# A decode kernel of two attention and two GLU layers: batches in two groups with K and V resident, K turned by VectorE

## The chip, the cores and the metric

The kernel runs on one core of a Trainium2 chip. All times are device microseconds (us) of one execution. A run more than 1.5% above the fastest of its kernel is called slow and is left out of the ratios. Medians are quoted over all runs, slow ones included, so where the two differ the ratio is to be trusted. "Granted clock" is the share of full speed at which TensorE's array clock runs, as the profile records it.

The profile names the engines PE (TensorE matmuls), PEld (TensorE weight loads), DVE (VectorE), ACT (ScalarE), POOL (GpSimd) and SPq (the queue of the sync engine, which issues all DMA here).

## The reference

Four tokens (batch 4, one position each, width 512) pass four layers: attention, GLU, attention, GLU. Both attentions use the same K and V caches and the same weights, and so do both GLUs.

```python
def attention(x):                       # x: [4, 1, 512]
    q = x @ wq                          # 32 heads of 128; 8 K/V heads, each shared by 4 query heads
    k, v = the last W = 2048 positions of k_cache, v_cache      # [4, 8, 2048, 128] each
    p = softmax(q k^T * 128 ** -0.5)
    return (p v) @ wo                   # [4096, 512]
def glu(x):
    return (sigmoid(x @ w_gate) * (x @ w_up)) @ w_down          # 512 -> 1792 -> 512
x = x + attention(layernorm(x)); x = x + glu(layernorm(x))
x = x + attention(layernorm(x)); x = x + glu(layernorm(x))
```

A (head, batch) pair has 512 KiB (0.52 MB) of K and as much of V; there are 32 pairs. K and V together are 33.6 MB. The kernel keeps an arena in on-chip memory of 49 slots of 512 KiB each, 25.7 MB, so K and V do not fit in it all at once. The second attention needs the result of the first for the same batch, but not for other batches: this is what the change uses.

## The kernel before

Every step is recorded as an operation with an engine, an assumed duration and the tiles that it reads and writes. A list scheduler then fixes the order on each engine, and semaphore waits are derived. Loads are issued in a fixed order; each takes the next free slot.

```python
# (cut) order of the layers
q_proj(0, ...)
for h in range(HKV):                    # first attention, all four batches of a head together
    if h + 1 < HKV: k_transpose(h + 1)
    scores_softmax(0, [h], QB, OB)
    pv_wo(0, h, keep)                   # V is dropped, K stays in its slots
glu(1)
q_proj(2, units2)
for hs in units2:                       # second attention: K is resident, V is loaded again
    scores_softmax(2, hs, 4, 5)
    ...
glu(3)
```

K is turned by TensorE transposes into PSUM, evacuated by VectorE and ScalarE in turn. In the scores, four neighbouring matmuls write to four column groups of the array (PSUM partitions 0, 32, 64, 96):

```python
for i, h in enumerate(heads):
    for b in range(NB):                 # b picks the column group
        pe.matmul(ps[32 * b:32 * b + rows, c, :], qt[:, q0:q0 + rows], K[h, b][:, c * 512:(c + 1) * 512], ...)
```

In the GLU, gate and up go to two PSUM banks, and each weight tile is one operation of 14 matmuls with four moving columns:

```python
for c in range(NC):
    for nm, bank in (("g", GB), ("u", UB)):
        P.op("tensor", ..., r=slot_tok(s) + [("xn",)], w=[("psg", bank)], banks=(bank,))
```

## Time and profile before

| | |
|---|---|
| time | 210.2 us (median of 3 runs; 208.6 to 211.6) |
| span of the profiled run | 207.9 us |
| read from HBM | 73.9 MB |
| PE / DVE / ACT busy | 69% / 35% / 32% |
| middle: end of attention 1 to first scores of attention 2 | 118.5 to 142.7 us, 24 us |
| end: end of attention 2 to the end of the span | 195.3 to 207.9 us, 12.6 us |

The first lines are the row of granted clock, the row of mean DMA busy share (both in tenths) and the GB/s moved, in 40 equal slices of 5.2 us, from the page of the kernel before:

```profile
PEclk9955588596699676969975555555555555555555
DMA  5999999999999999999997799999999999999300
GB/s 204 348 414 412 411 391 408 398 405 404 392 408 390 407 394 405 402 395 411 391 363 261 240 359 300 419 409 407 408 409 408 411 404 407 406 405 368 121 3 1
...
HBM read 73.93 MB, written 0.00 MB: 356 GB/s over the span
```

Outside three places (the start, the middle GLU in slices 21 to 25, the last four slices) DMA moves 390 to 419 GB/s. The kernel before is paced by its loads.

Some of the costliest groups of the same page (line, engine, operation, output and input tiles, shapes, count, then busy us and mean ns of one, then the idle time before them):

```profile
L526 PE MATMUL ps<-ident_b,arena 128*128 128x128 bf16 x512 | 48.5, 260 | 12.3 <-ACT arena L537 5.0
L537 ACT COPY arena<-ps 128x1024 bf16<-128x1024 bf16 x32 | 32.4, 1011 | 45.8 <-PE ps L526 45.8
...
L607 DVE TENSOR_REDUCE nmax<-ps 128x1 f32<-128x2048 f32 x12 | 27.5, 2290 | 11.8 <-PE ps L598 11.8
...
L598 PE MATMUL ps<-arena,qpad 128*8 128x512 bf16 x128 | 15.5, 617 | 0.8 <-DVE qpad L577 0.8
...
L598 PE MATMUL ps<-arena,qflat 128*4 128x512 bf16 x128 | 13.8, 481 | 0.5 <-DVE qflat L565 0.5
```

The transposes of K (L526) are the largest group. The 256 score matmuls (L598) are busy for 29.3 us together although one takes 481 or 617 ns: several run at once.

Two lines of the timeline: the middle GLU's gate and up, and the first score block of attention 2. A line gives start and duration in us, then instructions of one kind merged and their count, and in brackets the idle time of the engine before them and what ended it ("issue": nothing that the profile shows).

```profile
121.25 3.13 PE L710 MATMUL ps<-xn,arena 128*128 128x4 bf16 x112 [1.43 <-DVE xn L505]
...
142.68 3.59 PE L598 MATMUL ps<-arena,qpad 128*8 128x512 bf16 x32 [0.81 <-DVE qpad L577]
```

### The profile page before, as it was taken

To read this page: it belongs to the slowest core of one execution; us is meant where nothing else is said; L and a number is where in the kernel's file an instruction comes from. 1 tells how busy PE (TensorE), PEld (TensorE's weight loads), DVE (VectorE), ACT (ScalarE), POOL (GpSimd) and SP (SyncE) were. 2 spreads that over 40 slices of the span, in tenths; PEclk is the share of its full clock that TensorE was granted. 3 is DMA by queue.
4 is the path that set the end of the run, shared out by engine and by line. 5 is a ranking of instruction groups with operands and counts; after the bars stand their busy time and mean duration, and the time that the engine had idled before them with its cause. 6 is when DMAs were issued, how large, how long until landed. Compare 5 with 4: busy or idle time off the path is not lost.

```text
span 207.9 us, 6311 instructions
## 1 busy us (share of the span) xinstructions
PE 143.3 (69%) x2872; PEld 110.4 (53%) x2872; DVE 71.7 (35%) x155; ACT 67.1 (32%) x103; POOL 1.4 (1%) x9
## 2 busy tenths in 40 slices
PE   1684885969969499797756662547296972967564
PEld 1683554858657477675625662443054740546563
DVE  4410262363363534637435220201414204142221
ACT  2430146283584372938354010000314103131000
POOL 2000000000000000000000000000000000000000
PEclk9955588596699676969975555555555555555555
DMA  5999999999999999999997799999999999999300
GB/s 204 348 414 412 411 391 408 398 405 404 392 408 390 407 394 405 402 395 411 391 363 261 240 359 300 419 409 407 408 409 408 411 404 407 406 405 368 121 3 1
DMA packets 26409, 74.33 MB, mean 358 GB/s; under 512 B 2312, under 2 KB 10000, under 8 KB 26384
## 3 DMA queue, kind: packets, MB, share of 16 engines
q1 hardware_dynamic: 26384, 73.94, 92.6%
q8 instruction: 22, 0.36, 0.7%
q14 instruction: 3, 0.02, 0.0%
HBM read 73.93 MB, written 0.00 MB: 356 GB/s over the span
## 4 chain that ended last, share of the span: by engine, by line
PE 36%; SPq 24%; DMA 16%; DVE 12%; ACT 7%; issue 4%; ACTq 0%; DVEq 0%
SPq L367 24%; PE ps L598 10%; PE ps L659 9%; DVE nmax L607 8%; DMA arena<-in_A_k_cache_dram 8%; PE ps L526 7%; DMA arena<-in_A_wq_dram 5%; ACT prow L611 5%; DMA arena<-in_B_w_down_dram 4%; PE ps L684 2%; PE ps L619 2%; PE ps L710 2%; PE ps L639 2%; PE ps L740 1%; ACT arena L537 1%
## 5 line engine op out<-in xcount | busy, mean ns | idle before, releaser
L526 PE MATMUL ps<-ident_b,arena 128*128 128x128 bf16 x512 | 48.5, 260 | 12.3 <-ACT arena L537 5.0
L526 PEld LDWEIGHTS ps<-ident_b,arena 128*128 128x128 bf16 x512 | 39.4, 119 | 22.3 <-issue 10.5
L537 ACT COPY arena<-ps 128x1024 bf16<-128x1024 bf16 x32 | 32.4, 1011 | 45.8 <-PE ps L526 45.8
L611 ACT ACTIVATE prow<-ps,nmax 128x1024 bf16<-128x1024 f32 x24 | 26.6, 1113 | 46.7 <-DVE nmax L607 46.6
L659 PE MATMUL ps<-ebuf,arena 128*128 128x4 bf16 x1024 | 29.5, 166 | 7.4 <-DVE xT L691 5.2
L659 PEld LDWEIGHTS ps<-ebuf,arena 128*128 128x128 bf16 x1024 | 28.6, 102 | 11.1 <-issue 11.0
L607 DVE TENSOR_REDUCE nmax<-ps 128x1 f32<-128x2048 f32 x12 | 27.5, 2290 | 11.8 <-PE ps L598 11.8
L533 DVE COPY arena<-ps 128x1024 bf16<-128x1024 bf16 x32 | 22.1, 689 | 26.8 <-PE ps L526 26.8
L619 PE MATMUL ps<-sel_b,prow 128*128 128x16 bf16 (+1 forms) x192 | 8.9, 178 | 15.2 <-ACT prow L611 15.0
L619 PEld LDWEIGHTS ps<-sel_b,prow 128*128 128x128 bf16 x192 | 7.0, 101 | 21.9 <-ACT prow L611 17.9
L553 PE MATMUL ps<-xn,arena 128*128 128x4 bf16 x256 | 9.3, 167 | 10.4 <-DMA arena<-in_A_wq_dram 8.4
L598 PE MATMUL ps<-arena,qpad 128*8 128x512 bf16 x128 | 15.5, 617 | 0.8 <-DVE qpad L577 0.8
L553 PEld LDWEIGHTS ps<-xn,arena 128*128 128x128 bf16 x256 | 8.3, 105 | 11.6 <-DMA arena<-in_A_wq_dram 9.5
L598 PE MATMUL ps<-arena,qflat 128*4 128x512 bf16 x128 | 13.8, 481 | 0.5 <-DVE qflat L565 0.5
L671 DVE TENSOR_TENSOR onb<-ps,rinv 128x16 bf16<-128x16 f32 x16 | 3.1, 194 | 30.1 <-PE ps L659 30.1
L684 PEld LDWEIGHTS ps<-onb,arena 128*128 128x128 bf16 x256 | 8.4, 104 | 5.6 <-DVE onb L671 4.1
L684 PE MATMUL ps<-onb,arena 128*128 128x4 bf16 x256 | 9.3, 167 | 1.7 <-DVE onb L671 1.7
L499 ACT ACTIVATE lnv<-lnv 128x4 f32<-128x4 f32 x4 | 0.8, 205 | 27.3 <-DVE lnv L496 27.3
L710 PE MATMUL ps<-xn,arena 128*128 128x4 bf16 x224 | 6.3, 166 | 2.8 <-DVE xn L505 2.8
L740 PE MATMUL ps<-hT,arena 128*128 128x4 bf16 x112 | 4.1, 166 | 5.9 <-DMA arena<-in_B_w_down_dram 2.9
L710 PEld LDWEIGHTS ps<-xn,arena 128*128 128x128 bf16 x224 | 6.1, 104 | 3.0 <-issue 3.0
L629 ACT CAST ebuf<-ps 128x256 bf16<-128x256 f32 (+1 forms) x12 | 5.4, 449 | 6.9 <-PE ps L619 6.9
(45 smaller groups left out, 55.8 us busy)
## 6 DMA issues: line engine op xcount, KB each, us to landing
arena<-in_A_v_cache_dram SPq DMA_DIRECT2D x64, 512.0 KB, 12.3
arena<-in_A_k_cache_dram SPq DMA_DIRECT2D x32, 512.0 KB, 12.7
arena<-in_A_wq_dram SPq DMA_DIRECT2D x16, 512.0 KB, 10.8
arena<-in_A_wo_dram SPq DMA_DIRECT2D x8, 512.0 KB, 15.0
arena<-in_B_w_gate_dram SPq DMA_DIRECT2D x8, 448.0 KB, 12.4
arena<-in_B_w_up_dram SPq DMA_DIRECT2D x8, 448.0 KB, 9.4
arena<-in_B_w_down_dram SPq DMA_DIRECT2D x6, 512.0 KB, 9.6
arena<-in_B_w_down_dram SPq DMA_DIRECT2D x2, 256.0 KB, 7.5
```

The lines of the kernel that those rows point to most:

```text
L367: o = P.op("sync", name, 0.0, lambda e, dst=dst, src=src: e.dma_start(dst, src), r=r, w=w, dma_bytes=nbytes, dma_rate=tm[rate])
L526: last = pe.transpose(bankb(bank)[:, j * 128:(j + 1) * 128], half[:, j * 128:(j + 1) * 128], ident_b[:, :])
L533: lambda v, half=half, bank=bank: v.tensor_copy(half, bankb(bank)[:, 0:TB * 128]),
L537: lambda a, half=half, bank=bank: a.copy(half, bankb(bank)[:, 0:TB * 128]),
L553: last = pe.matmul(ps[:, QB, q * NB:(q + 1) * NB], src[:, k * 128:(k + 1) * 128], xn[:, c * NB:(c + 1) * NB], start=(st and k == 0), stop= ...
L598: last = pe.matmul(ps[32 * b:32 * b + rows, c, :], qt[:, q0:q0 + rows], slot_ap(s)[:, c * CH:(c + 1) * CH], start=(i == 0), stop=(i == ni ...
L607: lambda v: v.tensor_reduce(nm, ps[:, 0:NCH, :].rearrange("p c n -> p (c n)"), AXX, ALU.max, negate=True),
L611: lambda a, t=t: a.activation(prow[:, t * 1024:(t + 1) * 1024], ps[:, 2 * t:2 * t + 2, :].rearrange("p c n -> p (c n)"), ACTF.Exp, bias=nm ...
L619: last = pe.matmul(ps[:, ptb, j * n:(j + 1) * n], prow[:, j * 128:(j + 1) * 128], sel_b[:, 0:n], start=True, stop=True)
L659: last = pe.matmul(ps[:, OB, b * REP:(b + 1) * REP], src[:, j * 128:(j + 1) * 128], ebuf[:, c0:c0 + REP], start=(j == 0), stop=(j == NJ - 1))
L684: last = pe.matmul(ps[:, OB, 64 + c * NB: 64 + (c + 1) * NB], slot_ap(s)[:, r_ * D + c * 128:r_ * D + (c + 1) * 128], ov[:, r_ * NB:(r_ + ...
L710: last = pe.matmul(ps[:, bank, fc * NB:(fc + 1) * NB], src[:, fc * 128:(fc + 1) * 128], xn[:, c * NB:(c + 1) * NB], start=(c == 0 and fc = ...
```

## The change

The intent is to read V once. Batches are split into two groups, [0, 1] and [2, 3]. A group's K and V (16 pairs, 32 slots) stay resident through attention 1, GLU, and attention 2. The order becomes: attention 1 of group 0; GLU of group 0; attention 2 of group 0; attention 1 of group 1; GLU for both (the second of group 0, the first of group 1); attention 2 of group 1; last GLU. The price: the GLU weights are read three times instead of twice, and q is projected three times.

```diff
+        for gi, g in enumerate(GROUPS):            # [[0, 1], [2, 3]]
+            b0 = g[0] if gi == 0 else GROUPS[gi - 1][0]
+            attn(0, gi, WBS[0])
+            glu(gi, b0, g[-1] + 1)
+            layer_norm("Q%d" % gi, g[0], g[-1] + 1)
+            q_proj(gi + 1, g[0], g[-1] + 1)
+            attn(2, gi, WBS[1])
+        g = GROUPS[-1]
+        glu(NG, g[0], g[-1] + 1)
... (which weight tiles are loaded again at which use; the rest are kept in their slots)
+        again = dict(wq=[8, 4, 8], wo=[8, 0, 0, 0], glu=[12, 12, 12])
```

The second part: K is no longer turned on TensorE. VectorE transposes each K tile in place in 32x32 blocks of 4-byte words (pairs of bf16), and q is spread into a block-diagonal operand to fit. A unit is four pairs (two heads of two batches); its scores fill one PSUM bank.

```diff
-                        for j in range(TB):
-                            last = pe.transpose(bankb(bank)[:, j * 128:(j + 1) * 128],
-                                                half[:, j * 128:(j + 1) * 128], ident_b[:, :])
... (and the evacuations by VectorE and ScalarE)
+                v32 = slot_ap(s).bitcast(F32)
+                P.op("vector", "T%d_%d" % (h, b), c_dve(1024), lambda v, v32=v32: v.transpose(v32, v32), ...)
... scores: one operation per pair; the four matmuls of a pair all write to the pair's own column group
+            for gi, (h, b) in enumerate(pairs):
+                    kt = slot_ap(s).rearrange("p (j c k t) -> p c t j k", c=2, k=32, t=2)
+                    for cp in range(4):
+                        last = pe.matmul(ps[32 * gi:32 * gi + NR, bank, :], qbd[:, q0:q0 + NR],
+                                         kt[:, cp // 2, cp % 2, :, :], start=(cp == 0), stop=(cp == 3))
+                P.op("tensor", "S%s_%d_%d" % (tag, h, b), 4 * tm["pe_row"], e_s, ...)
... gate and up now share one PSUM bank and one token
-                    P.op("tensor", "gl%s%d_%d" % (nm, L, c), ..., w=[("psg", bank)], banks=(bank,))
+                    P.op("tensor", "gl%s%d_%d" % (nm, k, c), ..., w=[("cb",)], banks=(CB,))
```

## The prediction

> **What bounds the kernel now.** The page gives a span of 207.9 us with 73.9 MB read; away from the dips the slices move about 408 GB/s, so the DMA queue sets the pace. Its losses are the start (204, then 348 GB/s), the middle GLU (363, 261, 240 and 359 GB/s in slices 21 to 24) and the tail: in the timeline the last layer norm, GLU and output follow the last attention at 195.3 us and take 12.6 us.
>
> **Removed.** V is read once (16.8 MB less); wq grows by 4 loads of 0.52 MB, the GLU weights by a third pass (5.5 MB). Net: 64.7 MB, at 408 GB/s about 159 us instead of 181. The 512 TensorE transposes (48.5 us busy), their evictions (ACT 32.4, DVE 22.1), most of the 128x2048 maxima (27.5) and 192 small probability transposes go. Per K tile DVE gets one 128x1024 word transpose; the skill ("Vector Engine (DVE) Microarchitecture Reference", section 3.8) has one element per cycle per lane, so I estimate 1.15 us, 37 us in all, hidden.
>
> **Added, and decisive: the score matmuls.** Both kernels have 256 with 512 columns. Before, four neighbours go to four column groups and run together: in the timeline 32 of them take 3.59 us, four per 0.43 us, at granted clock 0.50 (0.22 us at 1.00); the next on the same group waits for that whole time. After, the order view shows the four of one (head, batch) pair accumulating into the same group, one after another; only the last of a pair can overlap the first of the next. A unit of four pairs thus costs about 13 x 0.43 = 5.6 us cold, 2.8 warm. With P.V (64 in 1.84 us), the output projection (32, about 1.2) and the small matmuls (about 1.2) a unit takes 10 us of TensorE cold, 7 warm, against 10.3 us for the eight loads it frees. There are 16 units.
>
> **Critical path.** First attention of group 0: DMA-paced, ends near 67 us. The 49 slots hold K, V, wo and part of wq, so the GLU and wq weights trickle through five: GLU and q projection until about 90 us. Then attention 2 of group 0 plus attention 1 of group 1, eight units, TensorE-bound: 56 to 82 us, where their loads alone need 41. GLU and q again, about 18 us. Attention 2 of group 1, four units with nothing left to load but the last GLU weights: 31 to 44 us, exposed. Last GLU and output: 12.5 us. Sum: 208 us warm to 247 cold; the clock will alternate[...]. I predict 222 us, range 204 to 243; faster 0.14, within 2% 0.14, slower 0.72.
>
> **What would show it.** HBM read 64.7 MB; DMA idle for some 40 us or more before the end; score matmuls of one pair starting 0.22 or 0.43 us apart; TensorE busy over 85% in the second attentions; the chain of waits mostly TensorE there; DMA dips around 67 to 90 us.
>
> **What would make it wrong.** If the score matmuls overlapped after all (0.1 us each), the units would be DMA-paced and the whole about 190 us. If the clock stays at 1.00 through the second attentions, about 205; if it stays at 0.50, near 245. If the word-strided moving operand reads slower[...], more.

## The result, and the profile after

The changed kernel takes 222.5 us (median of 4; 221.1 to 226.4) against 210.0 us (median of 4) of the kernel before: ratio 1.060, 95% interval 1.049 to 1.071, so it is slower by 6%. Ratios here are the mean time of one kernel's fast runs over that of the other's of the same rounds, so they are not quite the ratio of the medians quoted. The result is correct.

The profile of that first measurement fell in a slow run (226.4 us). The unchanged kernel was therefore run and profiled again (a_again below): 222.3 us, ratio 1.061, and a fast profiled run of 222.0 us with a span of 220.2 us. All lines "after" are from it. First clock, DMA share and GB/s in 40 slices, now of 5.5 us each:

```profile
PEclk9999995876955555557665559675555558755555
DMA  5999999999999899999999999800099999300000
GB/s 177 364 417 411 409 378 405 394 387 410 378 384 393 259 320 386 378 391 386 408 386 413 410 406 406 329 16 3 11 319 416 407 404 366 95 0 3 3 0 4
...
HBM read 64.75 MB, written 0.00 MB: 294 GB/s over the span
```

The bytes fell as planned, by 9.2 MB, which at 408 GB/s is about 22 us. But the DMA queue now stands still twice: in slices 27 to 29, and through the last five. The saving went into time in which nothing is left that may be loaded.

```profile
L626 PE MATMUL ps<-arena,qbd 128*16 128x512 bf16 x256 | 54.2, 539 | 13.5 <-DVE qbd L591 5.9
L607 DVE STREAM_TRANSPOSE arena<-arena 128x1024 f32<-128x1024 f32 x32 | 39.0, 1232 | 11.3 <-DMA arena<-in_A_k_cache_dram 11.0
...
L633 DVE TENSOR_REDUCE nmax<-ps 128x1 f32<-128x512 f32 x16 | 11.1, 692 | 22.4 <-PE ps L626 22.3
```

The transposes on TensorE are gone, and the 32 on VectorE (L607) cost 39 us of an engine that is busy for 41% of the span. The score matmuls, still 256 of 512 columns, are now busy for 54 us instead of 29.

The stages, read from the timelines (first and last matmul of each kind):

| stage | predicted, us | measured, us |
|---|---|---|
| attention 1 of group 0 ends | 67 | 69.8 |
| first middle section (layer norm, GLU, layer norm, q projection, q evacuation) | 23 | 28.1 (to 97.8) |
| eight attention units: attention 2 of group 0, attention 1 of group 1 | 56 to 82 | 57.0 (to 154.8) |
| second middle section | 18 | 23.8 (to 178.6) |
| attention 2 of group 1, four units | 31 to 44 | 27.0 (to 205.6) |
| last GLU and output | 12.5 | 14.6 (to 220.2) |

The total hit the prediction, but the stages show that this was in good part luck, two errors of opposite sign: the attentions were quicker than forecast and everything between them slower. Two views show both.

The second middle section, in the timeline of TensorE (cut to its matmuls; the first line is the end of the attention before it):

```profile
153.56 1.22 PE L704 MATMUL ps<-onb,arena 128*128 128x2 bf16 x32 [0.36 <-DVE onb L686]
155.49 0.59 PE L523 MATMUL ps<-lnr,ones_f 128*128 128x8 f32 x2 [0.71 <-DVE lnr L518]
157.51 5.13 PE L755 MATMUL ps<-xn,arena 128*128 128x4 bf16 x112 [1.43 <-DVE xn L546]
164.05 2.50 PE L783 MATMUL ps<-hT,arena 128*128 128x4 bf16 x56 [1.41 <-DVE hT L773]
167.23 0.59 PE L523 MATMUL ps<-lnr,ones_f 128*128 128x4 f32 x2 [0.68 <-DVE lnr L518]
...
173.46 0.56 PE L563 MATMUL ps<-xn,arena 128*128 128x2 bf16 x15 [0.81 <-DMA arena<-in_A_wq_dram]
174.96 1.61 PE L563 MATMUL ps<-xn,arena 128*128 128x2 bf16 x33 [0.94 <-issue]
177.10 0.40 PE L581 MATMUL ps<-qT,ident_b 128*32 128x64 bf16 x16 [0.53 <-DVE qT L571]
```

Gate and up (L755), the same 112 matmuls of the same shape as L710 before, take 5.13 us in place of 3.13. This section is about as long as the middle of the kernel before (23.8 against 24 us). Each step waits for the one before it, and it is a second passage of this kind beside the one that the kernel before had.

Attention 2 of group 1 (cut to some of its scores, L626, and output projections, L704):

```profile
178.57 3.63 PE L626 MATMUL ps<-arena,qbd 128*16 128x512 bf16 x32 [1.06 <-DVE qbd L591]
...
183.60 1.08 PE L626 MATMUL ps<-arena,qbd 128*16 128x512 bf16 x8
...
186.69 1.11 PE L626 MATMUL ps<-arena,qbd 128*16 128x512 bf16 x8
...
191.66 1.89 PE L626 MATMUL ps<-arena,qbd 128*16 128x512 bf16 x8
193.47 0.58 PE L704 MATMUL ps<-onb,arena 128*128 128x2 bf16 x16
193.99 1.87 PE L626 MATMUL ps<-arena,qbd 128*16 128x512 bf16 x4
...
204.35 1.22 PE L704 MATMUL ps<-onb,arena 128*128 128x2 bf16 x32 [0.36 <-DVE onb L686]
```

Read the counts against the times: 32 score matmuls take 3.6 us, 8 take 1.9 and 4 also take 1.9, all three at a granted clock of 0.50 (the blocks of 8 with 1.1 us fell in stretches at 1.00). So pairs run beside each other; four matmuls of one pair do not. The prediction had assumed that an operation issued later never runs beside the second or third matmul of an earlier pair. The single records agree: in the 32-block of the first profile, the four matmuls that end the four pairs of a unit (the only ones that raise a semaphore) start within 0.06 us of each other, at 100.90, 100.92, 100.94 and 100.96 us. (These starts are from the records of the packed trace; no view prints them one by one. The fast profile of a_again has the same picture, from 179.81 to 179.86 us, and there the four matmuls of one pair start 0.43 us apart.)

The Trainium skill says both things: "TensorEngine Tiling (Array Packing)", section Tiling Modes, has tiles that operate independently, which agrees with this trace; "TensorE: Matmul & The Clock Gate", Part 3, has matmuls start and end strictly in program order, which does not agree here.

What costs, then, is not the order within a block but a pair that stands alone (s_batch below tests this). The scheduler books four score matmuls at 0.32 us (4 x 0.08) and places them between other operations; there they take 1.9 us at a clock of 0.50.

### The profile page after: what moved, and what is told of

It reads as the page before. It is cut to its first block, busy times and chain, and to the rows that moved or that the text cites. A ratio compares the mean times of both kernels' runs of the same rounds, so it can differ in the third digit from the quotient of the medians.

```text
span 224.6 us, 6136 instructions
## 1 busy us (share of the span) xinstructions
PE 148.8 (66%) x2796; PEld 97.6 (43%) x2796; DVE 89.8 (40%) x219; ACT 19.4 (9%) x54; POOL 2.8 (1%) x8
## 3 DMA queue, kind: packets, MB, share of 16 engines
HBM read 64.75 MB, written 0.00 MB: 288 GB/s over the span
## 4 chain that ended last, share of the span: by engine, by line
PE 38%; SPq 24%; DMA 18%; DVE 11%; issue 4%; ACT 4%; ACTq 0%
SPq L364 24%; PE ps L626 16%; DMA arena<-in_A_wo_dram 6%; PE ps L674 5%; DMA arena<-in_A_wq_dram 5%; PE ps L755 4%; PE ps L704 4%; DMA arena<-in_B_w_down_dram 4%; DVE nmax L633 3%; PE ps L646 3%; DMA arena<-in_A_k_cache_dram 3%; ACT prow L642 3%; PE ps L783 2%; DMA arena<-in_B_w_gate_dram 2%; DVE arena L607 2%
## 5 line engine op out<-in xcount | busy, mean ns | idle before, releaser
L626 PE MATMUL ps<-arena,qbd 128*16 128x512 bf16 x256 | 55.0, 532 | 11.1 <-DVE qbd L591 5.9
L607 DVE STREAM_TRANSPOSE arena<-arena 128x1024 f32<-128x1024 f32 x32 | 38.9, 1231 | 12.1 <-DMA arena<-in_A_k_cache_dram 11.8
L626 PEld LDWEIGHTS ps<-arena,qbd 128*16 128x16 bf16 x256 | 14.2, 104 | 36.9 <-issue 19.5
L704 PEld LDWEIGHTS ps<-onb,arena 128*128 128x128 bf16 x512 | 16.4, 104 | 14.7 <-issue 6.9
L704 PE MATMUL ps<-onb,arena 128*128 128x2 bf16 x512 | 18.4, 165 | 6.5 <-DMA arena<-in_A_wo_dram 5.1
L563 PE MATMUL ps<-xn,arena 128*128 128x2 bf16 (+1 forms) x384 | 13.9, 166 | 12.6 <-DMA arena<-in_A_wq_dram 7.2
L633 DVE TENSOR_REDUCE nmax<-ps 128x1 f32<-128x512 f32 x16 | 11.0, 689 | 22.4 <-PE ps L626 22.3
L642 ACT ACTIVATE prow<-ps,nmax 128x512 bf16<-128x512 f32 x16 | 11.0, 687 | 103.2 <-DVE nmax L639 86.7
L755 PE MATMUL ps<-xn,arena 128*128 128x2 bf16 (+1 forms) x336 | 12.3, 165 | 10.5 <-DVE xn L546 4.2
L563 PEld LDWEIGHTS ps<-xn,arena 128*128 128x128 bf16 x384 | 12.2, 105 | 14.3 <-DMA arena<-in_A_wq_dram 8.1
L755 PEld LDWEIGHTS ps<-xn,arena 128*128 128x128 bf16 x336 | 10.9, 104 | 11.9 <-issue 8.1
L646 PE MATMUL ps<-prow,perm 128*128 128x512 bf16 x16 | 8.0, 498 | 9.2 <-ACT prow L642 9.1
L649 DVE STREAM_TRANSPOSE ebuf<-ps 128x512 f32<-128x512 f32 x16 | 11.3, 709 | 5.7 <-PE ps L646 5.6
L571 DVE TENSOR_SCALAR qT<-ps 128x64 bf16<-128x64 f32 (+1 forms) x3 | 1.6, 519 | 17.3 <-PE ps L563 17.3
L646 PEld LDWEIGHTS ps<-prow,perm 128*128 128x128 bf16 x16 | 1.6, 99 | 14.5 <-ACT prow L642 13.5
```

Of the source, the lines that this page charges most:

```text
L563: last = pe.matmul(ps[:, CB, q * nb:(q + 1) * nb], src[:, m * 128:(m + 1) * 128], xn[:, c * NB + b0:c * NB + b1], start=(c == 0 and q == 0 ...
L607: P.op("vector", "T%d_%d" % (h, b), c_dve(1024), lambda v, v32=v32: v.transpose(v32, v32), r=[("slot", s)], w=[("slot", s)])
L626: last = pe.matmul(ps[32 * gi:32 * gi + NR, bank, :], qbd[:, q0:q0 + NR], kt[:, cp // 2, cp % 2, :, :], start=(cp == 0), stop=(cp == 3))
L633: lambda v: v.tensor_reduce(nmax[:, k2:k2 + 1], ps[:, bank, :], AXX, ALU.max),
L642: lambda a: a.activation(prow[:, :], ps[:, bank, :], ACTF.Exp, bias=nmax[:, 2 + k2:3 + k2], scale=1.0, accum_out=psm[:, k2:k2 + 1]),
L646: lambda pe: pe.matmul(ps[:, PB, :], perm[:, :], prow[:, :], start=True, stop=True),
```

## The experiments

Twelve kernels ran. Each edit is against the changed kernel unless it says otherwise. All results were correct. "Section" is the time from the end of an attention to the first scores of the next.

### a_again: the changed kernel once more

No edit.

> The changed kernel unchanged, for a profile beside the other runs of this call. Theory 1 (the loss lies in TensorE-paced stages with the DMA queue idle: attention units, and GLU and q projection fed through few free slots) and every rival expect the same: about 222 us, 1.06 of the kernel before, DMA idle for over 35 us in sum after 145 us.

222.3 us (median of 4), ratio 1.061 (1.055 to 1.067). Mean DMA rates and engine busy times by stretch:

```profile
100.00:140.00 40.00, 34.47 (x622) 21.31 (x618) 26.29 (x57) 5.39 (x14) 0.00 (x0) 0.67 1.02 402
140.00:160.00 20.00, 15.52 (x334) 11.71 (x336) 5.01 (x20) 1.26 (x5) 0.00 (x0) 0.59 0.17 58
160.00:190.00 30.00, 19.65 (x439) 14.51 (x440) 8.88 (x30) 3.69 (x11) 0.00 (x0) 0.61 1.00 364
190.00:220.00 30.00, 21.30 (x450) 15.90 (x452) 6.41 (x26) 1.38 (x5) 0.00 (x0) 0.50 0.01 2
```

The columns are the stretch, its length, the busy us (and number) of PE, PEld, DVE, ACT and POOL, the granted clock, the DMA share and GB/s. DMA moves 58 GB/s from 140 to 160 us, which at 402 would have taken 2.9 us, and next to nothing in the last 30 us: about 17 + 30 = 47 us of idle queue, as expected.

### s_batch and s_inter: score matmuls of a unit in one block

In the second attentions, where all K tiles are there, one operation holds a unit's 16 score matmuls; s_inter also lets the column groups take turns.

```diff
-                P.op("tensor", "S%s_%d_%d" % (tag, h, b), 4 * tm["pe_row"], e_s, ...)      # one per pair
+            def e_sall(pe):
+                for gi, (h, b) in enumerate(pairs):       # s_batch: pair after pair
+                    for cp in range(4): last = s_mm(pe, gi, h, b, cp)
+            P.op("tensor", "S" + tag, 16 * tm["pe_row"], e_sall, ...)
... s_inter
+                for cp in range(4):
+                    for gi, (h, b) in enumerate(pairs): last = s_mm(pe, gi, h, b, cp)
```

> In the second attentions the 16 score matmuls of a unit are one block, still pair after pair (four matmuls to one column group, then four to the next). Theory 1a (column groups run side by side whatever the issue order, and what costs is a lone pair: four matmuls alone take 1.8 us while 32 in a row took 3.8): the lone blocks vanish, 16 take 1.0 to 1.9 us, total 3 to 7 us less, about 217. Rival 1b (the premise of the prediction: TensorE is in order, so only the last matmul of a pair overlaps the first of the next): a block of 16 takes 5.6 us cold or 2.8 warm and the total stays within 2 us of 222.

> As s_batch, but within the block the four column groups take turns, as in the kernel before. Theory 1a: issue order within the block does not matter, same time as s_batch within 1 us. Rival 1b: this one is faster than s_batch by 8 x (5.6 - 1.8) = 30 us cold, or 15 us warm.

s_batch: 216.0 us, ratio 1.030 (1.024 to 1.037). s_inter: 216.8 us, ratio 1.033 (1.026 to 1.040). In the same rounds the unedited kernel had 1.061. Two blocks of s_batch in the last attention, and one of s_inter (its profile fell in a slow run, 219.3 us), timelines of TensorE:

```profile
180.69 1.14 PE L621 MATMUL ps<-arena,qbd 128*16 128x512 bf16 x16
...
188.71 1.91 PE L621 MATMUL ps<-arena,qbd 128*16 128x512 bf16 x16
...
192.99 1.89 PE L621 MATMUL ps<-arena,qbd 128*16 128x512 bf16 x16
```

Sixteen matmuls take what four or eight took alone, and in s_batch the last attention falls from 27.0 to 22.8 us. That the order within the block makes no difference that these runs can tell decides between the two theories: column groups run side by side in both issue orders. The rival, on which the prediction's figure of 5.6 us per unit rested, asked for 15 to 30 us between the two. Two cautions. Of the later kernels, best5 and best6 each have one block of 16 that took longer, 2.92 us (at 180.51) and 2.76 us (at 176.26), at a clock of 0.50: part of its pairs started up to about 1 us after the others. No run explains it. And since pairs do not keep their order, a semaphore on the last matmul issued does not by itself say that the other pairs are done: in the block at 180.69 us a matmul of another pair has its start recorded 2 ns after that of the last one issued.

### wo_reload: free slots for the second middle section

```diff
-        again = dict(wq=[8, 4, 8], wo=[8, 0, 0, 0], glu=[12, 12, 12])
+        again = dict(wq=[8, 4, 8], wo=[8, 0, 0, 8], glu=[12, 12, 12])
```

> The eight wo tiles are loaded a second time for the last attention (4.2 MB more) instead of being kept, so their eight slots are free in the middle and the GLU and wq weights of the second group can be loaded during the attention before. Theory 2 (GLU and q projection are slow because their weights come through few slots): the stretch from the end of that attention to the scores of the last one falls from 24.5 us to about 15, total about 213 us in spite of 4.2 MB more. Rival (bytes decide): total 10 us longer, about 232 us.

223.3 us, ratio 1.067 (1.059 to 1.074). The expectation was missed. The q projection:

```profile
171.22 4.10 PE L563 MATMUL ps<-xn,arena 128*128 128x2 bf16 x95 [1.41 <-DVE xn L546]
176.40 1.61 PE L563 MATMUL ps<-xn,arena 128*128 128x2 bf16 x33 [1.07 <-issue]
```

It now took its first six wq tiles without a break and paused once, for 1.1 us, but the section took 23.3 us against 23.8: almost without waits for weights, the chain of dependent steps alone takes nearly as long. The rival that bytes decide was wrong too (it asked for 232).

### t_after_q: K transposes behind the q evacuation

The scheduler gives VectorE one fixed order of instructions, in which K transposes of the next group stood ahead of the evacuation of q. From the profile of the changed kernel (a_again), first middle section:

```profile
88.32 5.38 PE L563 MATMUL ps<-xn,arena 128*128 128x2 bf16 x128 [1.32 <-DVE xn L546]
92.68 1.25 DVE L607 STREAM_TRANSPOSE arena<-arena 128x1024 f32<-128x1024 f32 x1 [4.41 <-DMA arena<-in_A_k_cache_dram]
...
94.32 1.25 DVE L607 STREAM_TRANSPOSE arena<-arena 128x1024 f32<-128x1024 f32 x1 [0.39 <-DMA arena<-in_A_k_cache_dram]
95.49 0.40 DVE L571 TENSOR_SCALAR qT<-ps 128x64 bf16<-128x64 f32 x1
```

The projection ends at 93.7 us, but its evacuation (L571) starts at 95.5, behind a transpose that had waited for a K tile.

```diff
-                     r=[("slot", s)], w=[("slot", s)])
+                     r=[("slot", s)], w=[("slot", s)], after=[q_ev[max(q_ev)]] if max(q_ev) else [])
```

> VectorE's K transposes of the second group are made to wait for the q evacuation of the attention before them. In the profile of the change the evacuation stood behind transposes that waited for K tiles: q projection done at 95.1 us, first scores at 99.7. Theory 3 (a fixed order on VectorE puts a DMA wait into the critical chain): first scores about 3 us earlier, total about 219 us. Rival (those 3 us are absorbed by the loads that pace the units after it): within 1 us of 222.

221.3 us, ratio 1.054 (1.044 to 1.065). The section fell from 28.1 to 25.6 us, as expected. In the total the gain is about 1 us by the medians and is not separated from none: the intervals of 1.054 and 1.061 overlap. The transposes are thus not hidden everywhere, as the prediction had said; there was one place where they delayed the chain.

### wq_all: free slots for the first middle section

```diff
-        again = dict(wq=[8, 4, 8], ...)
+        again = dict(wq=[8, 8, 8], ...)
```

> All eight wq tiles are loaded again before the second attention of group 0 (2.1 MB more) in place of keeping four, so nine slots instead of five feed the first middle GLU. Theory 2 in its remaining form (in the first middle section the weights come late: the GLU matmuls wait for DMA seven times, in the second they do not): that section 3 to 6 us shorter, total 217 to 219 us. Rival (the serial chain of the section decides, as wo_reload showed for the second one): total within 1.5 us of 222, or longer by up to 5 us of DMA.

223.9 us, ratio 1.067 (1.058 to 1.076): no gain. The section took 27.3 us against 28.1: the GLU ended 1.5 us sooner (84.2 against 85.7), but the q projection then waited for the four added tiles until 94.7 instead of 93.7. In the unedited kernel DMA already averaged 385 GB/s from 80 to 100 us, so from there on more slots could do little but change the order in which bytes arrive.

### no_self: no waits of TensorE on itself

Gate and up share a bank and a token, so each operation of 14 matmuls waited until the one before it had ended. The edit drops waits of TensorE on its own earlier operations.

```diff
                 for d in o.deps:
+                    if e == "tensor" and d.eng == e:
+                        continue
```

> TensorE operations no longer wait on TensorE's own semaphore[...]. Theory 4 (the GLU and q sections are a serial chain, and part of it is new: gate and up share one bank, so each of the 8 chunks of 14 matmuls waits for the one before, 0.66 us instead of 0.39; the kernel before had them on two banks and 112 matmuls in 3.1 us): each GLU 2 us shorter, q projection 1 to 2 us, total 7 to 10 us less, about 213. Rival (weights arriving decide these sections): less than 2 us gain.

220.4 us, ratio 1.042 (1.026 to 1.058; only two of four runs were fast). The second middle section:

```profile
155.51 3.13 PE L757 MATMUL ps<-xn,arena 128*128 128x4 bf16 x112 [1.43 <-DVE xn L548]
...
172.84 0.59 PE L565 MATMUL ps<-xn,arena 128*128 128x2 bf16 x16 [0.69 <-DMA arena<-in_A_wq_dram]
174.13 0.58 PE L565 MATMUL ps<-xn,arena 128*128 128x2 bf16 x16 [0.70 <-DMA arena<-in_A_wq_dram]
```

Gate and up are back at 3.13 us, exactly the time of the kernel before, in this section and in the last (206.7 to 209.8). But the section still took 23.9 us: the q projection could begin 13.1 us after the attention's end instead of 14.5, and then waited for all but its first two wq tiles. The gain that shows is at the end of the kernel, from the last attention on: 11.8 us instead of 14.6. The edit does more than undo the shared bank: the 56 matmuls of the last down projection take 1.64 us instead of 2.50, and those waits were in the kernel before too.

### best1: four edits together

s_batch, t_after_q, wq_all and no_self.

> s_batch, t_after_q, wq_all and no_self together. If the four gains are in different stretches of the one chain they add: 222 - 6 - 3 - 4 - 8 = about 201 us, faster than the kernel before by 4%. If they overlap, about 207.

212.8 us, ratio 1.015 (1.002 to 1.028). The gains did not add to 201: wq_all gave nothing, and no_self gave nothing in the second section, which still took 23.6 us.

### early_and_free: no_self and wo_reload

Each alone had left the second section as it was, for the other's reason. This run has both edits and no other.

> no_self and wo_reload together. Alone they gained 2 us and nothing; in the second middle section (attention end to first scores, 23.8 us) wo_reload took the DMA waits away and the chain of dependent steps still took 23.3, no_self shortened the chain and the q projection then waited for wq until 174.7 us. Theory 5 (two limits of nearly the same length lie side by side there, so only removing both pays): section 17 to 18 us, last GLU 3 us shorter, total 211 to 213 us. Rival (something else fixes the section, for example the shared HBM rate): section still 23 us, total about 219.

212.2 us, ratio 1.013 (1.003 to 1.022), as expected. The profile is of a slow run (214.5 us); its section:

```profile
158.92 3.12 PE L757 MATMUL ps<-xn,arena 128*128 128x4 bf16 x112 [1.43 <-DVE xn L548]
163.46 1.63 PE L785 MATMUL ps<-hT,arena 128*128 128x4 bf16 x56 [1.41 <-DVE hT L775]
165.77 0.59 PE L525 MATMUL ps<-lnr,ones_f 128*128 128x4 f32 x2 [0.68 <-DVE lnr L520]
167.77 3.55 PE L565 MATMUL ps<-xn,arena 128*128 128x2 bf16 x128 [1.41 <-DVE xn L548]
173.32 3.63 PE L628 MATMUL ps<-arena,qbd 128*16 128x512 bf16 x32 [1.06 <-DVE qbd L593]
```

17.1 us instead of 23.8. By the ratios of fast runs to the kernel before, the unedited 1.061 becomes 1.067 with wo_reload alone (about 1 us more) and 1.042 with no_self alone (about 4 us less, on two fast runs); together it becomes 1.013, about 10 us less. Of these 10 us the section is 6.7 and the end 2.8. Two limits of nearly equal length lay side by side: the weights' arrival and the serial chain.

### best5: all edits that gave something

no_self, wo_reload, t_after_q, and score blocks of 16 in the first attentions too.

> no_self, wo_reload, t_after_q, and score blocks of 16 in both attentions. If theories 1a, 3 and 5 hold in different stretches: attention units 6 to 9 us less, first section 2 to 3, second section 6, last GLU 3: 202 to 205 us, 3% faster than the kernel before. If blocks of 16 in the first attentions wait too long for their fourth K tile, about 207.

205.1 us (median of 6), ratio 0.975 (0.966 to 0.984): faster than the kernel before by this interval, and about as expected. The stages: first section 24.4 us, eight units 52.7, second section 20.3, last attention 24.1, end 11.8. The granted clock is higher in this profile (mean 0.77 against 0.66 in a_again), but it does not carry the gain: the six runs of best6 below had mean clocks from 0.76 to 0.94 and agree within 1%, the two at 0.94 with 200.8 and 201.6 us.

### before_no_self: the same edit on the kernel before

> The no_self edit on the kernel before, to see whether that gain belongs to the grouped structure. The kernel before is paced by its loads except at its end: 1 to 2 us less there (down projection and the last gates), about 208.5 us. Rival (TensorE's waits on itself also hold back the loads through slot release): 4 us or more less.

207.9 us, ratio 0.994 (0.983 to 1.006): the same within the noise, so most of what no_self gives in combination belongs to the grouped structure, which has one more such section.

### best6: best5 with four wq tiles kept throughout

```diff
-        again = dict(wq=[8, 4, 8], wo=[8, 0, 0, 8], ...)
+        again = dict(wq=[8, 4, 4], wo=[8, 0, 0, 8], ...)
```

> best5 with four wq tiles kept throughout (2.1 MB less). In best5 the q projection of the second middle section still waited 2.9 us for its last wq tile behind a DMA queue that ran without a break. Theory (with TensorE's own delays gone the bytes decide again): that wait goes, total 201 to 203 us. Rival (four slots fewer hold back the K and V loads of the second group by as much): within 1 us of best5's 205.

201.6 us (median of 6; 200.6 to 202.5), ratio 0.967 (0.962 to 0.973). Its second section took 17.8 us against 20.3. That it beats best5 is likely but not settled: they ran in different calls and their intervals overlap (0.966 to 0.973). Clock, DMA and GB/s of its page:

```profile
PEclk9999999999999999999996555555555556955555
DMA  5999999999999978997999999999998999998000
GB/s 153 353 414 413 409 401 381 409 382 393 410 376 397 379 282 287 363 396 288 364 310 415 409 405 411 409 407 405 386 330 264 323 359 360 403 388 277 10 3 4
```

The hole in the middle is gone and the end is three slices of 5.0 us instead of five of 5.5. This is the grouped structure at work as it was meant: 66.9 MB, with DMA busy 91% of the span.

## Why the prediction was right, point by point

- **The total (222) and the direction** were right: 222.5 us, slower by 6%. The reason given, that TensorE-paced stages leave the DMA queue idle, is what the profile shows: about 47 us of idle queue after 140 us, "some 40 us or more" having been forecast.
- **The step that failed: "after, ... one after another; only the last of a pair can overlap the first of the next. A unit of four pairs thus costs about 13 x 0.43 = 5.6 us cold, 2.8 warm."** Sixteen score matmuls in a block took 1.1 us at a clock of 1.00 or 1.9 us at 0.50, so whole pairs overlapped. s_batch and s_inter showed that issue order within a block is of no account. What remains true is that four matmuls of one pair run one after another: alone they took 1.9 us, and the schedule scattered such lone pairs. That scatter was worth 6 us (222.3 to 216.0). The attentions therefore ran at the warm end of the forecast or below it (57.0 of 56 to 82; 27.0 of 31 to 44), although the mean clock was only 0.65 in the eight units and 0.63 in the last four.
- **The term that was mis-sized the other way: "GLU and q again, about 18 us"** (23.8), the first section (28.1 instead of 23) and the end (14.6 instead of 12.5). The prediction does not say how it came to 18; the same steps took 24 us in the kernel before, waits for weights included, and its 12.5 is the end of that kernel. The diff's shared bank made gate and up 2 us longer in the second and the last GLU (5.13 instead of 3.13), a cost that was there to be read. In the first GLU they waited for weights, and no run shows 2 us there; in that section the q evacuation stood behind K transposes, about 2.5 us.
- **"The 49 slots ... trickle through five"**: true as a description, but more slots alone gained nothing in either section (wo_reload, wq_all). In the second, slots paid only together with no_self.
- **"Per K tile DVE gets one 128x1024 word transpose; ... I estimate 1.15 us, 37 us in all, hidden"**: 1.23 us and 39.0 us. The skill's "Vector Engine (DVE) Microarchitecture Reference", section 3.8, with one element per cycle per lane, gave the right size. Hidden but for about 2.5 us at one place (t_after_q).
- **The signs to look for**: 64.75 MB was right; scores of one pair 0.41 to 0.43 us apart at the low clock was right; TensorE busy over 85% in the attentions was right (49.5 of 56.9 us in the eight units, 23.9 of 27.0 in the last four); the DMA dip was right (259 and 320 GB/s in slices 14 and 15).
- **What would make it wrong**: "If the score matmuls overlapped after all (0.1 us each), the units would be DMA-paced and the whole about 190." They did overlap, 0.11 us each in blocks, and the whole was 222. That sentence left out the scatter of lone pairs and the length of the sections. The hit on the total was luck to that extent, and no proof of the sum behind it: against the middle of each range (the middles add to 227), the last two attention stages came in 22.5 us shorter (12 and 10.5) and the other stages 15.8 us longer (2.8, 5.1, 5.8 and 2.1). (The other doubt, that the strided K might be read more slowly, did not come true: matmuls on one column group follow each other after 0.43 us at a clock of 0.50, as before.)

What stays open: why the granted clock is what it is in each stretch was not tested, and the remaining limit of the eight units (52.7 us in best5, where TensorE still waits at several places) was not taken apart. The change has two parts, the groups and the turning of K on VectorE with its block-diagonal q, and no run has one without the other, so what each is worth alone is not shown.

## What to carry to other kernels

Keeping data resident saves bytes, but it also bunches the work that needs no loads; before counting saved bytes as saved time, ask what the queue may load in each stage, and give it something there (here: wo dropped early and read again, 4.2 MB more, which cost nothing clear by itself and paid once TensorE's own waits were gone). When one remedy shows nothing, look in its profile for which wait took over: two limits of similar length hide each other, and only the run with both remedies tells. An operation that is cheap in a block and dear alone should be one block for the scheduler; that the booked 0.32 us was the reason for the scatter is likely, but no run changed this figure alone.

## What the Trainium skill lacked or had wrong

- "TensorE: Matmul & The Clock Gate", Part 3, says that matmuls keep program order strictly in start and end. Here the four closing matmuls of four pairs issued pair after pair started within 0.06 us of each other, and at a clock of 0.50 sixteen matmuls took 1.91 us pair after pair (s_batch) and 1.89 us in turns (s_inter). "TensorEngine Tiling (Array Packing)", section Tiling Modes, states the independence that fits; it has no figure for a lone group: four matmuls of 512 columns on one column group took 1.87 us, as long as sixteen on four groups (1.91).
- "TensorE: Matmul & The Clock Gate", Part 1, has activity raise the clock and idleness lower it. In best5 the granted clock was 1.00 from 15 to 70 us with TensorE busy 23 of 55 us, and 0.50 from 150 to 180 us with TensorE busy 20 of 30:

```profile
15.00:70.00 55.00, 23.23 (x489) 16.59 (x491) 30.48 (x48) 4.27 (x10) 0.00 (x0) 1.00 1.04 395
...
150.00:180.00 30.00, 20.28 (x504) 16.03 (x504) 9.73 (x33) 3.69 (x11) 0.00 (x0) 0.50 1.05 373
```

  The columns are as in the table of stretches above. Busy share as the profile counts it does not predict this clock, and one instruction stream does not fix it either (best6: run means from 0.76 to 0.94); no run here tells what does.
- No page was found that gives the cost of an operation of TensorE that waits on TensorE's own semaphore. Here eight such operations of 14 matmuls with four columns took 5.13 us, and 3.13 without the waits: about 0.29 us for each of the seven waits between them.
